# Expert weights prepared in half tiles, row factors stored as rows, and the preparation of the second layer moved, in a transform, mixture-of-experts and MLP kernel

## The chip, the cores and the metric

The kernel runs on one core of a Trainium2 chip. The metric is the device time of one execution in microseconds. Engines are named as the profile names them: PE (TensorE matmul), PEld (its weight loads), DVE (VectorE), ACT (ScalarE), POOL (GpSimd) and SP (SyncE, which here issues nearly all plain DMAs).

## What is computed

The reference takes x of 8 x 3072 x 256 and does three things in a row: a two-dimensional Fourier transform per batch of which the real part is kept, a mixture of eight experts with one expert per token, and a dense two-layer MLP.

```python
X = np.fft.fft(np.fft.fft(x, axis=1), axis=2).real          # 24576 tokens of 256
logits = x @ w_gate; expert_idx = argmax(logits)             # one expert of 8 per token
out[mask] = gate_w[mask, None] * (relu(xe @ w1[e]) @ w2[e])  # 256 -> 1024 -> 256
h = x @ w_in                                                 # 256 -> 2048
g = where(h >= 1, h, where(h <= -1, 0, (h + 1)**2 / 4))
return g @ w_out                                             # 2048 -> 256
```

## The kernel before

Matmuls of the two feed-forward parts run in fp16, each operand split into a high and a low half, so that one product is three matmuls. Everything that feeds them has first to be scaled by a power of two and split on ACT and DVE.

**Batches.** `all_batches` walks the eight batches. For each one `stage_a` (load x, fold it on DVE, transform on PE), `stage_db` for either half of the frequencies, and `route` for either half. `route` computes the gates, scales and splits the rows into `zsp` and `zsm` tiles and scatters them on POOL into the table `zd` in HBM, sorted by expert (`scatter`, line 564, 32 scatters in each batch). `table` then writes a list of tiles (`steps`): which rows of `zd`, which expert. A `yield` in these generators is one step of the main stream.

**Tiles of rows.** `Moe.run` takes the steps one by one. A tile has 128 to 512 rows. It is loaded transposed (`load_z`), goes through both expert layers in eight rounds of `l1` and `l2`, and each round yields twice, 16 yields a tile. The seven tiles of the first two batches (`PLAN[0]` four of 256 rows, `PLAN[1]` three of 512) are "raw": their expert weights are read as fp32 from the inputs and their matmuls run in fp32. All later tiles read split fp16 weights from `wd`, which `weights` writes. At the end of a tile `store` (line 811) sends the transposed result to `ytd` and the row factors `gs` (gate probability times scales, one number per row, one row per partition) to `gd`.

**Expert weights.** `weights` runs once, after the tables of batch 1 and before `stage_a` of batch 2. For each of eight experts it loads the two matrices (1 MB each) into three buffers borrowed from `xt` and `z`, takes the largest magnitude of one on DVE (line 270) and of the other by an accumulating ACT pass (line 274, its output goes to a `uv` buffer that nobody reads), makes the scales through two tiny matmuls (`all_max`), then makes four split pieces (lines 247 and 248) in the two `uv` buffers and stores each in `wd` (line 249). The load of a matrix waits until a whole earlier matrix has been split.

**MLP.** `Mlp.prep` prepares the dense layer's weights: for each of the two matrices 8 chunks (a load `mh`, then five DVE passes and three on `mlp.eng`, 5 yields), the largest magnitude, the scale, and 16 split steps: 66 yields for one matrix, 132 in all. `Mlp.run` works on blocks of 512 rows, 16 rounds of two yields, and can begin only when `prep` is over. `load` fetches a block (`ml`, `mg`), `factors` multiplies by the row factors on POOL (line 1018), `absmax` and the scales follow a block ahead.

**What sets the order.** SP's order is that of the program, the other engines' order is laid out at compile time from the same program. At the bottom (lines 1259 to 1296) the streams are interleaved by hand: until the first steps exist only the main stream and `prep` (0.3 of its steps for one main step, from the eleventh on) are drawn; then, as long as `prep` lasts, one tile yield is followed by `RAWF` main steps and `RAWP` prep steps (the first numbers until the steps of batch 1 exist, the second after that); then tile yields, MLP yields and main steps (1.25 after each of the two, 2.2 where no tile is ready). After the preparation PSUM gives the transform a single bank.

```python
                while not steps:
                    if len(fft.scattered) and mlp.eng is G:
                        mlp.eng = V
                    next(main)
                    i += 1
                    if i > PREPA:
                        ready(PREP0)
...
            while due[1]:
                i = len(steps) >= RAW
                if next(rows) == "wait":
                    forth(WAIT, 2)
                    ready(WAIT)
                else:
                    forth(RAWF[i], 2)
                    ready(RAWP[i])
```

Of the kernel before, what the change touches and what calls it, by code (L numbers as in the profile page):

```python
# [27 lines left out]
ZW = 258  # L28
# [20 lines left out]
RAWP = (0.7, 2.4)  # L49
# [109 lines left out]
def tile_kernel(ctx: ExitStack, tc: tile.TileContext, x, wg, w1, w2, win, wout,  # L159
# [56 lines left out]
    dis = [const.tile([128, 4], I32, name=f"di{i}") for i in range(NBLK)]  # L216
# [16 lines left out]
    def weights(pool, ps, later):  # L233

        def split(e, part, k, t):
            s = sct[:, e, part:part + 1]
            w = pool.tile([128, 2, 4, 128], F32, tag="uv", name="uv", bufs=2).rearrange("p a b c -> p (a b c)").bitcast(F16)
            w = w.rearrange("p (a b f) -> p a b f", a=2, b=2)
            if part == 0:

                src = t.rearrange("p (c f) -> p c f", c=2)[:, :, 512 * k:512 * k + 512]
                hi, lo = w[:, :, 0], w[:, :, 1]
            else:

                src = t.rearrange("p (j f) -> p j f", j=4)[:, 2 * k:2 * k + 2]
                hi, lo = w[:, 0], w[:, 1]
# [4 lines left out]
        ts = {}  # L251

        def load(j):
            if j >= 2 * E:
                return
            e, part = divmod(j, 2)
            t = pool.tile([128, 9 if j % 3 == 2 else 8, D], F32, tag=("xt", "xt", "z")[j % 3], name="wa", bufs=(2, 2, 1)[j % 3])
            t = ts[j] = t.rearrange("p a b -> p (a b)")[:, :2048]
            Y.dma_start(t.rearrange("p (c f) -> p c f", c=8 if part else 2), w2_view(e) if part else w1_view(e))

        load(0)
        load(1)
        store = None
        for e in range(E):
            for i in range(12 if e == 0 else 2):
                if e == 0 and i == 10:
                    load(2)
                yield
            am = pool.tile([128, 2], F32, name="wam", tag="wam", bufs=2)
            keep(V.tensor_reduce(am[:, 0:1], ts[2 * e], axis=AX.X, op=ALU.max, apply_absolute_value=True))  # L270
            yield

            ab = pool.tile([128, 2, 4, 128], F32, tag="uv", name="uv", bufs=2).rearrange("p a b c -> p (a b c)").bitcast(F16)
            keep(A.activation(ab, ts[2 * e + 1], AF.Abs, accum_out=am[:, 1:2]))
            for _ in range(4):
                yield
            pp = pool.tile([128, 2], F32, name="wpp", tag="wpp", bufs=2)
            for _ in all_max(am, 2, ps, later, pp):
                for _ in range(3):
                    yield  # L280
# [5 lines left out]
            for part in range(2):  # L286
                for k in range(2):
                    if store:
                        store()
                    store = split(e, part, k, ts[2 * e + part])  # L290
                    yield
                if part:
                    store()
                    store = None
                load(2 * e + part + 3)
# [381 lines left out]
    class Moe:  # L677
        def __init__(self, pool):
            self.pool = pool
            self.st = {}  # L680
            self.rows = self.stored = 0
            self.over = False
# [46 lines left out]
        def scale(self, n):  # L729
            st = self.st[n]  # L730
            nt, mt = st["nt"], st["mt"]
            st["gs"] = small.tile([128, 4], F32, tag="gs", name="gs", bufs=4)
            keep(V.tensor_scalar(st["gs"][:, :nt], mt[:, :, 1], st["sc"], None, op0=ALU.mult))
            if nt > 1:
                keep(V.tensor_copy(dis[st["blk"]][:, st["j"]:st["j"] + nt], mt[:, :, 0]))
# [143 lines left out]
    class Mlp:  # L879
# [117 lines left out]
        def load(self, t):  # L997
# [3 lines left out]
            if t < NBLK:  # L1001
# [4 lines left out]
                st["di"] = dis[t]  # L1006
# [160 lines left out]
    with tc.manual_schedule(engines={mybir.EngineType.SP}):  # L1167
# [37 lines left out]
        def all_batches():  # L1205
            yield from fft.stage_a(0)
            for b in range(B):
# [9 lines left out]
                if b == 1:  # L1217
                    yield from tables(b)
                    yield from weights(fpool, lambda shape: fft.ps("fb", shape), lambda fn: fft.later("w", fn))
# [27 lines left out]
        with tc.tile_pool(name="mlpp", bufs=1, side="right") as ppool:  # L1247
# [80 lines left out]
```

## Time and profile before

| | us |
|---|---|
| median of three runs | 3614.98 |
| the three runs | 3614.57, 3614.98, 3622.17 |
| the profiled execution | 3629.25 |
| its span | 3627.5 |
| PE busy in the span | 3389.2 |
| DVE, ACT, POOL busy | 2283.5, 1748.5, 1602.7 |

Busy time is the union of an engine's instructions; for PE the ends of matmuls are modelled. The profiled execution lies 14.3 us above the median of the runs. Its span is the sum of PE's busy time and PE's idle time, and the stages differ in how the two divide, so the views are read by stage. The cuts used below are moments of this execution: 47 is the first scatter of the first batch, 105 its last, 197 the last matmuls of the raw tiles of the first batch, 248 the end of the MLP's preparation, 336 the last raw matmul, 445 the last store of expert weights, 611 the first matmul of a tile with split weights.

### The profile page before, as it was taken

How to read it: one execution, taken by the hardware profiler on the slowest of the kernel's cores; microseconds unless marked ns; L12 is line 12 of the kernel's file. 1: busy time of each engine (PE TensorE's matmuls, PEld its weight loads, DVE VectorE, ACT ScalarE, POOL GpSimd, SP SyncE). 2: the span in 40 equal slices, each digit the busy share in tenths (PEclk: the TensorE clock that was granted, in tenths of full speed). 3: DMA queues.
4: the chain of work that ended last, by engine and by line, in shares of the span. 5: the costliest groups of instructions: out<-in, count | busy, mean ns of one | idle time of the engine just before them, and what ended most of it. 6: DMA issues, size and time to landing. Idle time of an engine off the chain costs nothing.

```text
span 3627.5 us, 60272 instructions
## 1 busy us (share of the span) xinstructions
PE 3389.2 (93%) x21741; PEld 2183.5 (60%) x21741; DVE 2283.5 (63%) x5137; ACT 1748.5 (48%) x3256; POOL 1602.7 (44%) x1399
## 2 busy tenths in 40 slices
PE   4778878998999999998999999999999999999999
PEld 4644545555565555555555566667777776666676
DVE  8566865676656666556544455566666666667676
ACT  3435644454444444444444444445444545555555
POOL 5442543343333433343432234344545445666555
PEclk7889988999999999999999999999999999999999
DMA  4677522544443533343444354344434441000000
GB/s 160 149 199 211 188 89 79 133 104 110 108 104 98 115 107 88 104 97 88 113 97 88 88 104 108 101 105 104 115 103 120 111 109 41 30 30 30 32 27 19
DMA packets 278608, 363.21 MB, mean 100 GB/s; under 512 B 172737, under 2 KB 193090, under 8 KB 275236
## 3 DMA queue, kind: packets, MB, share of 16 engines
q1 hardware_dynamic: 255028, 304.84, 33.2%
q0 software_dynamic: 23280, 54.52, 5.1%
q8 instruction: 171, 2.80, 0.3%
q14 instruction: 129, 1.06, 0.1%
HBM read 238.24 MB, written 95.87 MB: 92 GB/s over the span
## 4 chain that ended last, share of the span: by engine, by line
PE 70%; DVE 15%; issue 6%; DMA 3%; ACT 3%; POOL 2%; SPq 0%; another core or an unknown queue 0%; POOLq 0%; DVEq 0%; ACTq 0%
PE l L1057 21%; PE po L1086 18%; PE l L760 11%; PE py L799 9%; PE py L1086 4%; DVE r L1069 3%; DVE gf L1071 2%; ACT r L1068 1%; POOL g L1046 1%; DMA xt<-in_x 1%; PE py L780 1%; DMA wd<-uv 1%; PE f L425 1%; PE f L433 1%; DVE zam L520 1%
## 5 line engine op out<-in xcount | busy, mean ns | idle before, releaser
L1046 POOL TENSOR_TENSOR g<-gf,g 128x512 f16<-128x512 f32 (+1 forms) x784 | 925.9, 1182 | 1565.4 <-ACT g L1045 1525.8
L1057 PE MATMUL l<-yt,mw 128*128 128x512 f16 (+1 forms) x4704 | 1138.6, 377 | 23.7 <-issue 14.9
L1069 DVE SCALAR_TENSOR_TENSOR r<-r,bw 128x512 f32<-128x512 f32 (+1 forms) x784 | 657.8, 839 | 672.4 <-ACT r L1068 655.4
L1086 PEld LDWEIGHTS <-g 128*128 128x128 f16 x9216 | 898.5, 98 | 246.0 <-POOL g L1046 31.3
L1086 PE MATMUL po<-mw,g 128*128 128x256 f16 x7872 | 986.1, 274 | 26.9 <-POOL g L1046 23.0
L1068 ACT ACTIVATE r<-l,bw 128x512 f32<-128x512 f32 (+1 forms) x784 | 601.3, 767 | 549.2 <-PE l L1057 516.6
L1045 ACT CAST g<-gf 128x512 f16<-128x512 f32 (+1 forms) x784 | 474.9, 606 | 648.2 <-DVE gf L1071 620.6
L1057 PEld LDWEIGHTS <-mw 128*128 128x128 f16 x4704 | 457.4, 98 | 458.5 <-issue 46.5
L1071 DVE SCALAR_TENSOR_TENSOR gf<-l,bw,r 128x512 f32<-128x512 f32 (+1 forms) x784 | 577.4, 737 | 63.6 <-DVE r L1069 2.3
L760 PE MATMUL l<-zt,w 128*128 128x512 f16 (+2 forms) x3072 | 560.3, 318 | 27.3 <-DVE gf L1071 22.6
L799 PE MATMUL py<-h,w 128*128 128x512 f16 (+1 forms) x2064 | 472.9, 363 | 2.5 <-issue 2.5
L760 PEld LDWEIGHTS <-w 128*128 128x128 f16 x3072 | 272.2, 98 | 236.2 <-issue 43.5
L766 DVE SCALAR_TENSOR_TENSOR h<-l,h 128x512 f16<-128x512 f32 (+2 forms) x512 | 267.9, 523 | 224.0 <-ACT h L765 211.5
L765 ACT ACTIVATE h<-l 128x512 f16<-128x512 f32 (+2 forms) x512 | 238.1, 465 | 216.1 <-PE l L760 198.0
L799 PEld LDWEIGHTS <-w 128*128 128x128 f16 x2064 | 201.4, 98 | 181.7 <-issue 6.4
L1102 POOL DMA_INDIRECT out<-mo,di x178 | 189.1, 1062 | 89.4 <-ACT mo L1094 43.5
L564 POOL DMA_INDIRECT zd<-zsp,pi x136 | 147.2, 1083 | 171.5 <-ACT zsm L557 41.6
L1086 PE MATMUL py<-mw,g 128*128 128x256 f16 x1344 | 165.0, 273 | 0.0
L1018 POOL TENSOR_TENSOR ml<-ml,mg 128x512 f32<-128x512 f32 (+1 forms) x90 | 120.4, 1353 | 77.7 <-DMA mg<-gd 56.5
L564 POOL DMA_INDIRECT zd<-zsm,pi x120 | 124.3, 1036 | 53.9 <-issue 28.3
L796 PE MATMUL py<-h,w 128*128 128x256 f32 (+1 forms) x224 | 82.3, 493 | 17.0 <-ACT h L755 10.2
L754 PE MATMUL l<-zt,w 128*128 128x256 f32 (+1 forms) x224 | 84.6, 504 | 13.3 <-DVE zt L825 13.3
(256 smaller groups left out, 2491.9 us busy)
## 6 DMA issues: line engine op xcount, KB each, us to landing
w<-wd SPq DMA_DIRECT2D x256, 512.0 KB
ml<-yt SPq DMA_DIRECT2D x44, 512.0 KB
yt<-y SPq DMA_DIRECT2D x78, 256.0 KB
xt<-in_x SPq DMA_DIRECT2D x16, 1024.0 KB
wa<-in_w SPq DMA_DIRECT2D x16, 1024.0 KB
wd<-uv SPq DMA_DIRECT2D x32, 512.0 KB
w<-in_w SPq DMA_DIRECT2D x28, 512.0 KB
mg<-gd SPq DMA_DIRECT2D x44, 256.0 KB
```

The costliest lines, as they stand in the source:

```text
L564: i = G.indirect_dma_start(out=zd[:, :], out_offset=bass.IndirectOffsetOnAxis(ap=idx, axis=0), in_=rows, in_offset=None, bounds_check=ZROW ...
L760: P.matmul(ph, w[:, c, a, sl], zt[:, zz, c, :m], start=k == 0, stop=k == 5)
L765: A.activation(hi, ph, AF.Relu)
L766: V.scalar_tensor_tensor(lo, ph, 0.0, hi, op0=ALU.max, op1=ALU.subtract)
L799: P.matmul(st["py"][c], w[:, a, o + 128 * c:o + 128 * c + 128], h[:, r, :m], start=f == 0 and k == 0, stop=f == 7 and k == 2)
L1045: A.copy(hi, gf)
L1046: G.tensor_tensor(lo, gf, hi, op=ALU.subtract)
L1057: P.matmul(ph, w[:, a, sl], yt[:, b, c, :m], start=k == 0, stop=k == 5)
L1068: A.activation(r, ph, AF.Relu, bias=st["b1"], scale=st["c1"])
L1069: V.scalar_tensor_tensor(r, r, st["mc"], r, op0=ALU.min, op1=ALU.mult)
L1071: V.scalar_tensor_tensor(gf, ph, st["c2"], r, op0=ALU.mult, op1=ALU.max)
L1086: P.matmul(po, g[:, a, js], w[:, b, sl], start=f == 0 and k == 0 and j % 2 == 0, stop=f == 15 and k == 2, skip_group_check=True)
```

## The change

- **Row factors.** `gs` becomes one of four lasting 128 x 32 tiles that are cleared once. After the factors are computed in its first columns, DVE transposes it in blocks of 32 into `gt`, so that factors of 32 partitions lie in one row; `store` then writes them with four DMAs of rows of 32 numbers in place of one DMA of single numbers. The row indices `dis` become one tile in place of one per block.
- **Expert weights.** The three buffers become eight slots of half a matrix (six in `xt` and `z`, two in the transform's `au`). The load, the magnitude and the split go by halves. The magnitudes of an expert alternate with the splits of the expert before it; a half is loaded two experts ahead as soon as its slot has been split. The unread output of the magnitude pass goes to a `zsp` buffer instead of `uv`. Counted in the code, the generator has 122 yields in place of 154.
- **Preparation.** None between the first scatter of the first batch and its table. After that 1.0 and 3.0 prep steps for a tile yield in place of 0.7 and 2.4; the three passes of `mlp.eng` run on DVE until the steps of batch 1 exist and on POOL after that (before: DVE during the first batch's scatters, POOL otherwise).

```diff
-RAWP = (0.7, 2.4)
+RAWP = (1.0, 3.0)
...
+        slots = []
+        for tag, n, w in (("xt", 2, 8), ("xt", 2, 8), ("z", 1, 9)):
+            v = f1(pool.tile([128, w, D], F32, tag=tag, name="wa", bufs=n), 2)
+            slots += [v[:, 0], v[:, 1]]
+        slots += [a.rearrange("d g s c -> d (g s c)")[:, :1024] for a in fft.au]
...
+            if e < E:
+                k, part = divmod(i, 2)
+                t = slots[(4 * e + i) % 8]
+                if part == 0:
+                    Y.dma_start(t.rearrange("p (c f) -> p c f", c=2), w1_view(e)[:, :, 512 * k:512 * k + 512])
+                else:
+                    Y.dma_start(t.rearrange("p (c d) -> p c d", c=4), w2_view(e)[:, 4 * k:4 * k + 4])
...
+        for i in range(4):
+            load(0, i)
+        yield
+        for i in range(4):
+            load(1, i)
+            yield
...
+        for e in range(E + 1):
+            am = pool.tile([128, 2, 2], F32, name="wam", tag="wam", bufs=2)
+            for i in range(4):
+                if e < E:
+                    src = slots[(4 * e + i) % 8]
+                    if i % 2 == 0:
+                        keep(V.tensor_reduce(am[:, i // 2, 0:1], src, axis=AX.X, op=ALU.max, apply_absolute_value=True))
+                    else:
+                        keep(A.activation(ab, src, AF.Abs, accum_out=am[:, i // 2, 1:2]))
                 yield
+                if store:
+                    store()
+                    store = None
+                if e > 0:
+                    store = split(e - 1, i)
+                    yield
+                    load(e + 1, i)
...
-            st["gs"] = small.tile([128, 4], F32, tag="gs", name="gs", bufs=4)
+            st["gs"] = self.gs[n % len(self.gs)]
...
+                st["gt"] = small.tile([128, 32], F32, tag="gt", name="gt", bufs=2)
+                keep(V.transpose(st["gt"], st["gs"]))
...
-            Y.dma_start(gd[blk][0, o:o + m].rearrange("(j p) -> p j", p=128), st["gs"][:, :nt])
+            for b in range(4):
+                Y.dma_start(gd[blk][0, o:o + m].rearrange("(j b q) -> b j q", b=4, q=32)[b], st["gt"][32 * b:32 * b + nt])
...
-                    if len(fft.scattered) and mlp.eng is G:
-                        mlp.eng = V
                     next(main)
                     i += 1
-                    if i > PREPA:
+                    if i > PREPA and not fft.scattered:
                         ready(PREP0)
...
-            mlp.eng = G
             while due[1]:
                 i = len(steps) >= RAW
+
+                mlp.eng = G if i else V
```

## Rows read from the trace of the kernel before

**Rows 1.** The page, PE's busy share in 40 slices of the span (tenths):

```profile
PE   4778878998999999998999999999999999999999
```

**Rows 2.** Busy time by stage: stretch, its length, each engine, granted clock, DMA:

```profile
47.00:105.00 58.00, 26.11 (x117) 22.38 (x116) 52.17 (x182) 23.54 (x65) 48.37 (x32) 0.56 0.35 109
105.00:197.00 92.00, 71.70 (x348) 61.09 (x349) 56.74 (x236) 42.10 (x126) 39.24 (x35) 0.89 0.71 165
197.00:248.00 51.00, 33.97 (x83) 16.75 (x82) 30.54 (x45) 12.27 (x22) 30.02 (x22) 0.80 0.86 221
248.00:336.00 88.00, 79.60 (x258) 36.37 (x257) 54.25 (x107) 44.91 (x61) 15.92 (x12) 0.96 0.69 207
336.00:445.00 109.00, 89.81 (x545) 54.85 (x544) 91.07 (x132) 68.78 (x94) 50.10 (x36) 0.96 0.56 177
445.00:611.00 166.00, 126.29 (x791) 86.20 (x790) 106.50 (x306) 77.39 (x169) 84.90 (x75) 0.88 0.26 84
611.00:911.00 300.00, 277.59 (x1556) 159.79 (x1556) 187.80 (x484) 138.16 (x284) 108.60 (x101) 0.96 0.50 119
911.00:3627.00 2716.00, 2659.15 (x17896) 1722.71 (x17893) 1671.65 (x3553) 1325.62 (x2395) 1216.17 (x1075) 1.00 0.34 86
```

**Rows 3.** POOL in order of time, 45 to 110, start, length, and idle before:

```profile
47.18 1.78 POOL L564 DMA_INDIRECT zd<-zsm,pi  x1 [10.55 <-ACT pd L428]
...
84.90 4.97 POOL L564 DMA_INDIRECT zd<-zsm,pi  x1 [0.30 <-issue]
...
104.28 0.92 POOL L564 DMA_INDIRECT zd<-zsm,pi  x1 [0.30 <-issue]
```

**Rows 4.** Groups of DVE instructions by line, 45 to 108 (the preparation's):

```profile
L922 DVE TENSOR_REDUCE mam<-mr 128x1 f32<-128x1024 f32 x4 | 4.8, 1207 | 0.0
...
L918 DVE TENSOR_TENSOR mr<-mr,mm 128x512 f32<-128x512 f32 x6 | 4.1, 682 | 0.0
...
L911 DVE TENSOR_SCALAR mp<-mu 128x512 uint32<-128x512 uint32 x5 | 2.1, 414 | 0.0
```

**Rows 5.** Groups of POOL instructions by line, 130 to 206 (the second batch's scatters):

```profile
L564 POOL DMA_INDIRECT zd<-zsp,pi x17 | 18.8, 1106 | 48.2 <-ACT zsp L545 38.3 <-DVE zsp L540 5.8 <-issue 3.7
L564 POOL DMA_INDIRECT zd<-zsm,pi x15 | 14.3, 953 | 4.4 <-issue 3.8 <-ACT zsp L545 0.3 <-ACT zsm L557 0.3
...
L917 POOL TENSOR_TENSOR mr<-mr,mu 128x512 f32<-128x512 f32 x3 | 3.8, 1278 | 0.5 <-DVE mr L915 0.5
```

**Rows 6.** Who waited for whom, 105 to 255: total, times, longest:

```profile
DVE mu L908 <- DMA mh<-in_wout: 16.9, 2, 16.2
...
PE l L754 <- DVE zt L825: 13.3, 1, 13.3
```

**Rows 7.** The chain that ended last, 105 to 245: start, us, what:

```profile
160.80 5.11 DMA mh<-in_wout
197.99 14.57 DMA mh<-in_wout
```

**Rows 8.** The chain that ended last, 240 to 460: the stores of expert weights on it:

```profile
260.60 8.19 DMA wd<-uv
291.94 9.70 DMA wd<-uv
...
335.99 10.44 DMA wd<-uv
```

**Rows 9.** What SP's queue waited for, 230 to 620:

```profile
SPq L249 <- DVE uv L248: 126.1, 21, 12.1
SPq L1004 <- DVE yt L1037: 53.1, 1, 53.1
```

**Rows 10.** Instructions on the row factors `gs`: duration ns min/median/max, first and last start:

```profile
L733 DVE TENSOR_SCALAR gs<-mt,stb x64: 192/217/1756, 615.4 to 2998.8; 128x4 f32<-128x4 f32 x36, 128x1 f32<-128x1 f32 x21, 128x2 f32<-128x2 f32 x7
L816 SPq DMA_DIRECT2D gd<-gs x50: 346/454/936, 137.1 to 2988.0; - x50
```

**Rows 11.** What SP's queue waited for in the whole span, the longest total:

```profile
SPq L723 <- PE py L799: 718.2, 74, 23.8
```

More of the change, by code (lines that the diff above doesn't have):

```diff
@@ L215, in tile_kernel @@
     onesf = const.tile([128, 128], F32, name="onesf")
-    dis = [const.tile([128, 4], I32, name=f"di{i}") for i in range(NBLK)]
+    dis = const.tile([128, NBLK, 4], I32, name="dis")
     V.memset(onesf, 1.0)
@@ L231, in w2_view, with weights, load, split @@
         return w2[e].rearrange("(c p) d -> p c d", p=128)
-    def weights(pool, ps, later):
-        def split(e, part, k, t):
+    def weights(fft, ps, later):
+        pool = fft.pool
+        f1 = lambda t, n: t.rearrange("p a b -> p (a b)")[:, :1024 * n].rearrange("p (n f) -> p n f", n=n)
+        slots = []
[3 more added lines that the diff above has]
+        slots += [a.rearrange("d g s c -> d (g s c)")[:, :1024] for a in fft.au]
+        def load(e, i):
+            if e < E:
[5 more added lines that the diff above has]
+                    Y.dma_start(t.rearrange("p (c d) -> p c d", c=4), w2_view(e)[:, 4 * k:4 * k + 4])
+        def split(e, i):
+            k, part = divmod(i, 2)
             s = sct[:, e, part:part + 1]
+            src = slots[(4 * e + i) % 8].rearrange("p (a f) -> p a f", a=2)
             w = pool.tile([128, 2, 4, 128], F32, tag="uv", name="uv", bufs=2).rearrange("p a b c -> p (a b c)").bitcast(F16)
             w = w.rearrange("p (a b f) -> p a b f", a=2, b=2)
[L239 to L246, printed above, removed]
+            hi, lo = (w[:, :, 0], w[:, :, 1]) if part == 0 else (w[:, 0], w[:, 1])
             A.activation(hi, src, AF.Copy, scale=s)
@@ L249, in split @@
             return lambda: Y.dma_start(wd[e, part, k], w.rearrange("p a b f -> p (a b f)"))
[L251 to L259, printed above, removed]
@@ L261, in weights @@
-        load(0)
-        load(1)
-        store = None
[L264 to L267, printed above, removed]
-                yield
-            am = pool.tile([128, 2], F32, name="wam", tag="wam", bufs=2)
-            keep(V.tensor_reduce(am[:, 0:1], ts[2 * e], axis=AX.X, op=ALU.max, apply_absolute_value=True))
+        for i in range(4):
[4 more added lines that the diff above has]
+            yield
@@ new lines, in weights @@
+        ab = pool.tile([128, 3, ZW], F32, tag="zsp", name="zsp", bufs=3).rearrange("p a b -> p (a b)")[:, :512].bitcast(F16)
+        store = None
+        for e in range(E + 1):
[7 more added lines that the diff above has]
+                        keep(A.activation(ab, src, AF.Abs, accum_out=am[:, i // 2, 1:2]))
+                yield
+                if store:
[5 more added lines that the diff above has]
+                    load(e + 1, i)
+            if e == E:
+                break
+            a2 = pool.tile([128, 2], F32, name="wa2", tag="wa2", bufs=2)
+            V.tensor_tensor(a2, am[:, 0], am[:, 1], op=ALU.max)
@@ L271, in weights @@
             yield
-            ab = pool.tile([128, 2, 4, 128], F32, tag="uv", name="uv", bufs=2).rearrange("p a b c -> p (a b c)").bitcast(F16)
-            keep(A.activation(ab, ts[2 * e + 1], AF.Abs, accum_out=am[:, 1:2]))
-            for _ in range(4):
+            pp = pool.tile([128, 2], F32, name="wpp", tag="wpp", bufs=2)
+            for _ in all_max(a2, 2, ps, later, pp):
                 yield
[L277 to L280, printed above, removed]
+                yield
@@ L285, in weights @@
             yield
[L286 to L295, printed above, removed]
+        store()
+        yield
     class Fft:
@@ L681, in __init__ @@
             self.rows = self.stored = 0
+            self.gs = [const.tile([128, 32], F32, name=f"gs{i}") for i in range(4)]
+            for t in self.gs:
+                V.memset(t, 0.0)
             self.over = False
@@ L731, in scale @@
             nt, mt = st["nt"], st["mt"]
-            st["gs"] = small.tile([128, 4], F32, tag="gs", name="gs", bufs=4)
+            st["gs"] = self.gs[n % len(self.gs)]
             keep(V.tensor_scalar(st["gs"][:, :nt], mt[:, :, 1], st["sc"], None, op0=ALU.mult))
             if nt > 1:
-                keep(V.tensor_copy(dis[st["blk"]][:, st["j"]:st["j"] + nt], mt[:, :, 0]))
+                keep(V.tensor_copy(dis[:, st["blk"], st["j"]:st["j"] + nt], mt[:, :, 0]))
+                st["gt"] = small.tile([128, 32], F32, tag="gt", name="gt", bufs=2)
+                keep(V.transpose(st["gt"], st["gs"]))
             else:
@@ L1005, in load @@
                 Y.dma_start(st["gr"][:, :m], gd[t][:, :m].to_broadcast([128, m]))
-                st["di"] = dis[t]
+                st["di"] = dis[:, t]
             else:
@@ L1218, in all_batches @@
                     yield from tables(b)
-                    yield from weights(fpool, lambda shape: fft.ps("fb", shape), lambda fn: fft.later("w", fn))
+                    yield from weights(fft, lambda shape: fft.ps("fb", shape), lambda fn: fft.later("w", fn))
                     fft.load_x(b + 1, 0)
```

## Prediction

> **What bounds the kernel now.** I read the 40 slices first, then busy time by stage, and after that only the stages with a gap. PE is at nine tenths or more from the eleventh slice on [rows 1]; from 911 to the end it works 2659.2 of 2716 us at full clock [rows 2]. Since the span is PE's busy time and PE's idle time, 3389.2 + 238.3, and the change takes no matmul of weight away, the sum below goes by PE's idle time alone. By stage it is: up to 47, 22 (47 less the 25.0 that the other stages leave of 3389.2); 47 to 105, 31.9; 105 to 197, 20.3; 197 to 248, 17.0; 248 to 336, 8.4; 336 to 445, 19.2; 445 to 611, 39.7; 611 to 911, 22.4; after that 56.9 [rows 2]. The reader is to see there that all three edits with any weight touch the first 445 us, and that each stage waits for something else.
>
> From 47 to 105 PE has little to do; the first batch's 32 scatters run on POOL almost without a break, 0.30 us apart, from 47.2 to 105.2, but they last 0.92 us at best and up to 4.97 us [rows 3]. DVE is busy 52.2 of the 58 us [rows 2], over half of it with the MLP's preparation: nine groups from 4.8 to 2.1 us, in sum 28.9 us [rows 4]. From 105 to 248 the raw tiles, the second batch and the rest of the preparation share DVE, and DMA is busy 0.71 to 0.86 of the time [rows 2]; DVE stood 16.9 us for two loads of the preparation, PE 13.3 us for the sum of a raw tile's halves on DVE [rows 6], and those two loads, 5.1 and 14.6 us, lie on the chain [rows 7]. From 248 to 445 the expert weights are made; four stores of pieces, from 8.2 to 10.4 us and one of 3.0, in sum 31.4 us, lie on the chain [rows 8], because the next user of a `uv` buffer waits until its store has landed.
>
> **The change part by part.**
>
> *A. No preparation between the first batch's scatters.* Main steps counted in the code: 171 until the first table, 55 until the first scatter. At 0.3 from the eleventh on, 48 prep steps lie there now and 13 will; 35 move behind. Without DVE's 28.9 us, 23.3 us of DVE are left in the stretch [rows 2, 4], ACT has 23.5 and PE 26.1 [rows 2]; so POOL's scatters at their best pace, 32 x (0.92 + 0.30) = 39.0 us, are what is late next. That is 19.0 us under the 58.0 measured. The second batch's scatters, with less DVE work beside them, lasted (18.8 + 14.3) / 32 = 1.03 us [rows 5], which gives 32 x 1.33 = 42.6 us and a gain of 15.4. Bounds: 8 (half, if the 13 steps that stay drag into the scatters) to 19. I take 16: the row of the second batch is the nearest.
>
> *B. The moved steps.* 35 prep steps are 7 chunks' worth of work, of which the absolute maxima are a part; chunk loads behind 105 go from 8 to about 13. The second rate is 3.0, so prep ends after about 73 tile yields (50 x 1.0 + 23 x 3.0 on top of 13) where it now ends after 71 (50 x 0.7 + 20.4 x 2.4 on top of 48). Mlp's first block therefore starts at the same place in the program. DVE gets 28.9 us more between 105 and 248, where it has 35.3 + 20.5 = 55.8 us free [rows 2]; that is the cover. If it were gone the cost would be all 28.9. POOL is relieved of prep passes between the second batch's scatters (three passes of 1.3 us [rows 5] between the last of them), so the low bound is -4. Between them I go by the row on what the preparation costs there today: 16.9 us of DVE waiting for 8 chunks [rows 6], 2.1 each, and 5 more chunks: +10.
>
> *C. Expert weights.* Five uses of the two `uv` buffers for an expert become four, and between two splits there is now a magnitude pass of the next expert, so a store has one pass more in which to land. Loads come by halves, two experts ahead. The generator takes 122 main steps in place of 154; the MLP rounds that no longer fit beside it are done later and are PE work either way. So the gain is PE's idle time from 248 to 445, 8.4 + 19.2 = 27.6 us, and at most the clock's loss on top, 0.04 x 169.4 = 6.8 us [rows 2]. The chain's 31.4 us of stores says the same size [rows 8]. Bounds 8 (one of the four stores gone) to 35; I take 24, most of the idle time, as a chain of splits remains. The change adds a wait: SP stands at each load until its slot has been split, with the tiles' weights, the MLP's block loads and the stores queued behind it. It already stands 126.1 us in 21 waits at the stores for the same DVE pass [rows 9], so the new wait takes the place of the old one: 0, bounds 0 to +10.
>
> *D. What follows.* The second transform (445 to 611) has one PSUM bank and is paced by its own latencies. Its 39.7 us of PE idle, and the 53.1 us that SP stood at one block load until DVE had freed the block [rows 9], are not touched: 0, bounds -12 to +12 as the loads fall otherwise.
>
> *E. Row factors.* 50 transposes: a DVE pass over four columns takes 0.217 us [rows 10], one over 512 columns 0.68 us [rows 4], so 11 to 34 us of DVE in all, of which nearly everything lies behind 611, where DVE is idle 1156 us [rows 2]. 50 stores of 0.454 us become 200: 68 us more on SP [rows 10], which stands 718.2 us for one kind of wait alone [rows 11]. Nothing of either is on the path: 0, bounds -5 (blocks get their factors sooner) to +5. The single index tile, the clears and the `zsp` buffer are counted at nothing: one write a tile, as before.
>
> On E the Trainium skill speaks against the change: "DMA: Bandwidth & Descriptors", section "Rules for kernel authors", says that a DMA whose outermost dimension is below 16 is confined to at most that many DMA engines, and these have four rows or two. Its section "Specifications" puts about 0.6 us of latency ahead of the first byte of a DMA from SP; by that 150 more DMAs, one behind the other on the path, would be 90 us and the time 3675. No row here shows SP or PE waiting for a store of factors.
>
> **Sum.** -16 + 10 - 24 + 0 + 0 = -30 us. The profiled span of 3627.5 becomes 3597.5. The profiled execution is 14.3 us above the median of the runs, so the median of 3615 becomes 3585.
>
> **The rivals.**
>
> *Slower: the preparation outruns its loads.* In the second half of the raw tiles 8 chunks are asked for in 13 tile yields, two buffers deep, behind raw weights and 4 MB of expert weights that are now asked for at once, where DMA is already 0.86 busy [rows 2]. If DVE stood for each of the eight at the mean of the two rows, (5.1 + 14.6) / 2 = 9.9 us [rows 7], that is 79 us in place of 16.9, and as DVE runs in order the sums of raw tiles and the second batch stand behind it. Then B is +62 in place of +10: -16 + 62 - 24 = +22, 3637. It decides from 57 us of DVE waiting for `mh` on (16.9 and the 40 that A and C bring). For it: PE's 13.3 us wait. Against: six of the eight chunks today cost nothing visible.
>
> *The stretch moves to the second batch.* DVE's passes lengthen POOL's scatters; in the first raw tiles 50 prep steps, now with all passes on DVE, run beside the second batch's 32 scatters. If these went from 1.03 us to the first batch's 48.6 / 32 = 1.52 us (POOL's 48.4 us busy [rows 2] and a remainder at the edge), 32 x 0.49 = 16 us come back, since PE's wait of 13.3 us is for the first tile of that batch [rows 6]: -14, 3601. The Trainium skill, "SBUF — State Buffer", section "SBUF: two separate sides", says why it could be so: while DVE holds the port pair that it shares with GpSimd, the latter cannot write descriptors. The long scatter between 84.9 and 89.9 [rows 3] agrees.
>
> *Given back.* The second transform keeps its distance to a block load that comes late, as the one of 53.1 us did [rows 9]; the 30 us turn into idle time between 445 and 611: 3615.
>
> *More.* The weights' stage ends early enough that the second transform meets fuller MLP work, and a third of the 39.7 + 22.4 us idle from 445 to 911 goes too [rows 2]: -30 - 21 - 9 (B at +1) = -60, 3555.
>
> *It doesn't do what it says:* the compiler's order might put preparation between the scatters all the same. That is A at 0 with B at 0, -24: 3591, inside the forecast's own range.
>
> **How the numbers follow.** Forecast, 3565 to 3600: 0.42. More: 0.13. The stretch moves: 0.15. Given back: 0.12. Slower: 0.18. 0.2% is about 7 us, what a measurement of this kernel can tell from no change. Faster is 0.42 + 0.13 + 0.15 = 0.70, same 0.12, slower 0.18. The range goes from 3545, past the center of "more", to 3633, just short of the center of the slower case; about 0.05 is left out below and 0.10 above. The forecast's own range with its bounds (A 8 to 19, C 8 to 35) is 3560 to 3608.
>
> **What would show it.** A: the last of the first 32 scatters ends near 90 (right: 86 to 92), each near 1 us. B: DVE's wait for `mh` under 30 us, and the MLP's first round no more than 10 us later than before. C: `wd` stores under 15 us on the chain, and the last store of weights 30 to 55 us before 445. D: from the last store to the first split-weight matmul 166 us as before. E: no wait that names `gd`, `gt` or `gs` beyond a few us. I would be wrong if DVE stood over 57 us for `mh`, if the second batch's scatters averaged 1.5 us, or if the distance from the last weight store to the first split-weight tile grew by 20 us or more.

## The result and the profile after

| | before | after |
|---|---|---|
| median of the runs, us | 3614.78 | 3566.96 |
| lowest to highest | 3613.76 to 3622.17 | 3565.16 to 3568.72 |
| ratio, 95% interval | | 0.9863 [0.9846, 0.988] |
| span of the profiled execution | 3627.5 | 3562.8 |
| PE busy, PE idle in it | 3389.2, 238.3 | 3377.1, 185.7 |

The kernel became 48 us faster by the medians, 1.37% by the ratio. The forecast was 3585, with a range from 3545 to 3633. The number held; most of its reasons did not, as the experiments show. The two profiled executions lie 65 us apart, more than the medians, because that of before was itself 14 us above its median.

The page of after: span, busy time of PE, PE's slices (they answer [rows 1]), packets, and the queue of SP's DMAs.

```profile
span 3562.8 us, 60571 instructions
...
PE 3377.1 (95%) x21741; PEld 2183.5 (61%) x21741; DVE 2303.6 (65%) x5207; ACT 1752.5 (49%) x3272; POOL 1592.2 (45%) x1399
...
PE   5778788999999999999999999999999999999999
...
DMA packets 259777, 363.21 MB, mean 102 GB/s; under 512 B 150833, under 2 KB 171186, under 8 KB 257428
...
q1 hardware_dynamic: 236196, 304.84, 29.8%
```

The bytes are what they were, 363.21 MB, but there are 18,831 packets fewer (278,608 before), and the time that SP's packets took fell from 33.2% of the engines' span to 29.8%.

Busy time of after by stage, cut at the moments that answer those of [rows 2]: the columns are length, then PE, PE's weight loads, DVE, ACT, POOL, granted clock, DMA share and GB/s.

```profile
47.00:91.00 44.00, 27.53 (x153) 24.14 (x152) 32.60 (x147) 25.15 (x75) 33.78 (x32) 0.75 0.33 97
91.00:187.00 96.00, 73.00 (x331) 61.60 (x332) 64.68 (x252) 41.59 (x120) 35.08 (x32) 0.88 0.68 198
187.00:248.00 61.00, 44.40 (x102) 19.68 (x100) 50.50 (x80) 16.61 (x28) 37.64 (x26) 0.83 0.60 184
248.00:312.00 64.00, 59.36 (x203) 27.93 (x204) 43.09 (x85) 38.56 (x59) 11.87 (x9) 1.00 0.80 255
312.00:407.00 95.00, 74.71 (x450) 45.51 (x449) 81.00 (x125) 59.89 (x85) 37.69 (x29) 0.96 0.62 208
407.00:588.00 181.00, 146.47 (x884) 99.52 (x882) 126.19 (x335) 88.71 (x184) 93.27 (x80) 0.88 0.24 76
588.00:888.00 300.00, 288.15 (x1669) 168.21 (x1670) 194.96 (x507) 147.85 (x298) 120.35 (x108) 1.00 0.44 125
888.00:3562.00 2674.00, 2638.68 (x17803) 1713.82 (x17800) 1678.36 (x3577) 1318.89 (x2384) 1213.19 (x1071) 1.00 0.31 87
```

PE's idle time by stage is 16.5, 23.0, 16.6, 4.6, 20.3, 34.5, 11.9 and 35.3 us, where before had 31.9, 20.3, 17.0, 8.4, 19.2, 39.7, 22.4 and 56.9. The forecast looked for its 30 us ahead of 445. There the scatters' stretch gives 15.4, and the four stages behind it 0.4 together. The transform gives 5.2, the 300 us after it 10.5, and the long rest 21.6, where neither the preparation nor the expert weights are at work any more. The only edit that still acts there is the one of the row factors, counted at nothing. PE's busy time fell by 12.1 us with the same 21741 matmuls; in the 300 us after the transform the granted clock is 1.00 where it was 0.96. Counted by PE's matmuls, after leads before by 12 us at the 800th (286 us into before), 16 at the 1400th (425), 22 at the 2400th (635), 39 at the 4000th (937), 61 at the 9000th (1833) and 65 at the end.

The row factors of after: the four stores a tile (SP) and the transposes (DVE); count, then shortest, median and longest in ns, and first and last start. They answer [rows 10].

```profile
L835 SPq DMA_DIRECT2D gd<-gt x200: 228/320/1157, 131.9 to 2924.3; - x100
L753 DVE STREAM_TRANSPOSE gt<-gs x50: 189/211/214, 99.7 to 2889.1; 128x32 f32<-128x32 f32 x50
```

SP's part is 200 x 0.32 = 64 us in place of 50 x 0.454 = 23, and the transposes are 10.6 us of DVE. So the edit adds work on both engines, and yet the stretch in which it acts became shorter.

### The profile page after: what moved, and what is told of

The parts are those of the page before. It is cut to its first block, busy times and chain, and to the rows that moved or that the text cites. A ratio compares the mean times of both kernels' runs of the same rounds, so it can differ in the third digit from the quotient of the medians.

```text
span 3562.8 us, 60571 instructions
## 1 busy us (share of the span) xinstructions
PE 3377.1 (95%) x21741; PEld 2183.5 (61%) x21741; DVE 2303.6 (65%) x5207; ACT 1752.5 (49%) x3272; POOL 1592.2 (45%) x1399
## 2 busy tenths in 40 slices
DMA packets 259777, 363.21 MB, mean 102 GB/s; under 512 B 150833, under 2 KB 171186, under 8 KB 257428
## 3 DMA queue, kind: packets, MB, share of 16 engines
q1 hardware_dynamic: 236196, 304.84, 29.8%
q14 instruction: 131, 1.07, 0.1%
## 4 chain that ended last, share of the span: by engine, by line
PE 72%; DVE 13%; issue 5%; DMA 4%; ACT 3%; POOL 3%; SPq 0%; POOLq 0%; DVEq 0%; ACTq 0%
PE l L1076 22%; PE po L1105 18%; PE l L778 11%; PE py L817 10%; PE py L1105 4%; DVE r L1088 3%; DVE gf L1090 2%; POOL g L1065 1%; DMA wd<-uv 1%; ACT r L1087 1%; PE f L421 1%; PE py L798 1%; DMA zd<-zsm,pi 1%; POOL zd L576 1%; DVE zam L532 1%
## 5 line engine op out<-in xcount | busy, mean ns | idle before, releaser
L1088 DVE SCALAR_TENSOR_TENSOR r<-r,bw 128x512 f32<-128x512 f32 (+1 forms) x784 | 667.0, 851 | 657.4 <-ACT r L1087 655.8
L778 PE MATMUL l<-zt,w 128*128 128x512 f16 (+2 forms) x3072 | 556.7, 316 | 14.2 <-DVE gf L1090 11.9
L1121 POOL DMA_INDIRECT out<-mo,dis x178 | 187.8, 1055 | 93.5 <-ACT mo L1113 47.7
L1056 DVE SCALAR_TENSOR_TENSOR yt<-ml,bw,yt 128x512 f16<-128x512 f32 (+1 forms) x90 | 74.4, 845 | 28.5 <-ACT yt L1055 28.3
```

The costliest lines, as they stand in the source:

```text
L778: P.matmul(ph, w[:, c, a, sl], zt[:, zz, c, :m], start=k == 0, stop=k == 5)
L1088: V.scalar_tensor_tensor(r, r, st["mc"], r, op0=ALU.min, op1=ALU.mult)
```

## The experiments

They ran in three sets on three chips, each beside the kernel before on the same chip (medians 3624.01, 3632.79 and 3614.18). Ratios are to those; times of different sets are only compared through them. Even so a comparison across sets can be off by more than its interval: the kernel before differs by 19 us from chip to chip, while the kernels with the rows lie close together on two of them (3566 for the rows alone on one, 3563 and 3567 with more reads and with spread numbers on the other).

**Which part carries the gain.** Four kernels: the preparation's new order alone (A and B of the prediction), the expert weights alone (C), the rows alone (E), and everything but the rows.

*The rows alone:* the index tile, the lasting `gs`, the transpose and this store.

```diff
-            Y.dma_start(gd[blk][0, o:o + m].rearrange("(j p) -> p j", p=128), st["gs"][:, :nt])
+            for b in range(4):
+                Y.dma_start(gd[blk][0, o:o + m].rearrange("(j b q) -> b j q", b=4, q=32)[b], st["gt"][32 * b:32 * b + nt])
```

> The kernel before with the row factors' part alone: lasting gs tiles, DVE transposes, four row DMAs a tile, one index tile. Theory (the parts add up, and the row factors are worth nothing): 3610 to 3620 us, within 0.2% of the kernel before. Rival (the PE idle time that went after the first split-weight tile, 32 us between the two profiles, is the row factors'): 3575 to 3600 us, with POOL waiting less for mg and PE's idle time after 611 down from 79 to about 50 us.

Measured: 3565.74 us (3561.32 to 3567.82), ratio 0.9838 [0.9822, 0.9854], below even the rival's range. The whole gain is here. PE's idle time is 189.8 us in place of 238.3. At PE's matmuls its lead over before is 27 us at the 1400th (425 us into before), 30 at the 2400th, 41 at the 4000th, 61 at the 9000th and 64 at the end, so that less than half of it comes ahead of the 445 us in which the forecast looked.

*The preparation's order alone:*

```diff
-RAWP = (0.7, 2.4)
+RAWP = (1.0, 3.0)
...
-                    if len(fft.scattered) and mlp.eng is G:
-                        mlp.eng = V
...
-                    if i > PREPA:
+                    if i > PREPA and not fft.scattered:
...
+                mlp.eng = G if i else V
```

> The kernel before with the preparation's part alone: none between the first batch's scatters, 1.0 and 3.0 steps after that, its three passes on DVE until the second batch's steps exist. Theory: the last of the first 32 scatters ends near 91 instead of 105 us, and about 10 us of the 14 are lost again while the raw tiles share DVE and DMA with the moved steps: 3605 to 3612 us. Rival 1 (the whole 14 us arrive at the end): 3600 us. Rival 2 (all given back in the raw tiles): 3615 us or more, with the MLP's first round no earlier than 278 us.

Measured: 3641.12 us, ratio 1.0047 [1.0031, 1.0063]. As the second rival had it, 3615 or more; that rival does not say why the kernel is 17 us slower than before and not level with it.

*The expert weights alone* (with one line more, `fft.flush("w")`, that issues the stage's pending work ahead of the scales; the change has no such line):

```diff
-    def weights(pool, ps, later):
+    def weights(fft, ps, later):
...
+        slots += [a.rearrange("d g s c -> d (g s c)")[:, :1024] for a in fft.au]
...
+            fft.flush("w")
             sc = sct[:, e]
```

> The kernel before with the expert weights' part alone: halves through eight slots, 122 main steps in place of 154 (and one flush of pending evacuations ahead of the scales). Theory: this is the largest part, 3580 to 3595 us, the last weight store 25 to 40 us earlier than 445. Rival (the stage ends earlier but the time is lost between the last store and the first split-weight tile): last store as early, that distance longer than 162 us by 20 or more, time 3605 or more.

Measured: 3636.78 us, ratio 1.0036 [1.0022, 1.0051]: slower too, as the rival had it, though with smaller distances than it named. The line `fft.flush("w")` was not run by itself, so its price is not known.

*Both without the rows:* the diff of the change without the five places that name `gs`, `gt` and `dis`.

> The changed kernel with the row factors as before (single numbers in one DMA, no transpose): preparation and weights parts together. Theory: 3562 to 3572 us, the changed kernel's time, as the row factors are worth nothing. Rival (the row factors matter in the steady stretch): 3580 to 3600 us.

Measured: 3628.54 us, ratio 1.001 [1.0, 1.0019]. Neither theory nor rival: the two edits on which the forecast stood make no difference of use.

**What in the rows.** A look back at the chain of before gave the theory. Three DMAs on it last 13 us and more, and each is under way behind a store of factors: those stores start at 137.1 (0.1 us after the first of the three), 190.6 and 838.4. First the chain of before at two places (the third of them, a load of 14.57 us at 197.99, is in [rows 7]), then SP's queue at the later one:

```profile
137.03 13.12 DMA zd<-zsp,pi
...
838.89 13.97 DMA xt<-in_x
```

```profile
838.39 0.44 SPq L816 DMA_DIRECT2D gd<-gs  x1
838.89 1.37 SPq L380 DMA_DIRECT2D xt<-in_x  x2
```

In the kernel with the rows alone the load of `xt` on the chain between 760 and 860 takes 6.74 us. The old store writes 512 numbers of 4 bytes for a large tile, 22,872 more 4-byte packets in the whole trace than with rows (44,229 to 21,357), and the new one pieces of 128 bytes. The two kernels side by side, 2 us each, from 2 us behind the third store on: GB/s is the last column, the busy share of the DMA engines the one ahead of it. A packet's whole time is booked in the slice in which it starts, so that a share can pass 1.

Before, store at 190.6:

```profile
192.60:194.60 2.00, 2.00 (x8) 1.61 (x7) 2.00 (x8) 0.82 (x4) 1.52 (x3) 0.69 1.25 66
194.60:196.60 2.00, 2.00 (x11) 1.77 (x10) 1.80 (x16) 0.38 (x1) 1.70 (x2) 1.00 1.04 41
196.60:198.60 2.00, 2.00 (x11) 1.77 (x10) 0.00 (x0) 0.38 (x1) 1.68 (x3) 1.00 1.18 41
198.60:200.60 2.00, 2.00 (x11) 1.77 (x10) 0.00 (x0) 0.51 (x2) 1.83 (x2) 1.00 0.62 33
```

The rows alone, store at 178.8:

```profile
180.80:182.80 2.00, 2.00 (x11) 1.77 (x10) 2.00 (x11) 0.61 (x2) 1.97 (x2) 1.00 0.69 142
182.80:184.80 2.00, 2.00 (x11) 1.75 (x10) 1.16 (x11) 0.38 (x1) 1.63 (x2) 1.00 0.95 385
184.80:186.80 2.00, 2.00 (x11) 1.76 (x10) 0.00 (x0) 0.38 (x1) 1.59 (x2) 1.00 1.03 368
186.80:188.80 2.00, 2.00 (x11) 1.77 (x10) 0.00 (x0) 0.38 (x1) 1.67 (x3) 1.00 1.06 381
```

The reader is to see that the DMA engines count as busy in both (1.18 and 1.03), while 41 GB/s go through in the one and 368 in the other. A busy share says only that packets are under way. From this came the theory that the large packets behind the store are held up.

*The old store beside the new one,* into a tensor that nothing reads:

```diff
+            Y.dma_start(gx[blk][0, o:o + m].rearrange("(j p) -> p j", p=128), st["gs"][:, :nt])
```

> The kernel with the rows alone (3566 us), and the old store number by number kept beside the new one, into a tensor that nothing reads. Theory (the 4-byte writes of a factor store hold up what is queued behind them on the DMA engines): the gain goes again, 3608 to 3632 us, and large packets behind these stores are as slow as in the kernel before. Rival (the gain comes from the lasting factor tiles, the single index tile, or from factors that land sooner): still 3560 to 3574.

Measured: 3641.11 us, ratio 1.0029 [1.0009, 1.005], against the 0.9838 of the rows alone. The store by single numbers takes the whole gain back by itself; nothing that the new layout brings makes up for it.

*The rest of the edit without its store:* lasting `gs` and one index tile, but the old store.

> The lasting factor tiles and the single index tile alone, without the transpose, and with the old store number by number. Theory: nothing of the gain is here, 3608 to 3632 us. Rival (they carry the gain, since a small tile's turn no longer waits for an old store): 3560 to 3580.

Measured: 3629.06 us, ratio 0.9999 [0.9986, 1.0013]. The tiles are worth nothing; the rival falls.

*The same bytes in fewer pieces:*

```diff
-            Y.dma_start(gd[blk][0, o:o + m].rearrange("(j p) -> p j", p=128), st["gs"][:, :nt])
+            Y.dma_start(gd[blk][0, o:o + m].rearrange("(p j) -> p j", p=128), st["gs"][:, :nt])
```

> The kernel before with one store of factors a tile as before and the same bytes, but partition by partition: 128 writes of 16 bytes in place of 512 of 4. The factors so land in another order, and the sum at the end weighs rows with each other's factors; the work is otherwise the same. Theory, if the price goes by the number of writes: a quarter of the 58 us is left, 3570 to 3592 us. Rival, if it goes by the store as such or by its bytes: 3610 to 3632, as before.

Measured: 3584.42 us, ratio 0.9875 [0.9844, 0.9906]. As expected: one DMA a tile as before, 2 KB as before, 128 writes in place of 512, and about three quarters of the gain is there (by the intervals, from a half to nearly all). The price is that of small writes, not of the store.

*A second dose:* the kernel before, with the line that `rows_plus_numbers` adds (a store of single numbers into `gx`) behind its own store.

> The kernel before with the store of the factors number by number made twice, the second into a tensor that nothing reads. Theory: a second dose of the same hold-up, 30 to 65 us on top of the kernel before, 3645 to 3690 us. Rival (the store itself costs nothing): within 8 us of the kernel before.

Measured: 3638.96 us, ratio 1.0029 [1.0013, 1.0046], some 10 us on top (5 to 17 by the interval) where 30 to 65 were expected. The theory in this form fell: twice the writes don't hold up twice as long. The window behind one store shows it. In before, 6 us behind the store at 1038.7:

```profile
1044.70:1046.70 2.00, 2.00 (x11) 0.94 (x10) 0.03 (x1) 1.05 (x2) 1.16 (x1) 1.00 0.00 0
1046.70:1048.70 2.00, 2.00 (x13) 1.02 (x12) 1.27 (x2) 0.78 (x1) 0.00 (x0) 1.00 1.76 33
1048.70:1050.70 2.00, 2.00 (x17) 1.49 (x15) 1.18 (x3) 0.62 (x1) 0.28 (x1) 1.00 0.39 33
1050.70:1052.70 2.00, 2.00 (x12) 1.08 (x10) 0.61 (x1) 0.60 (x2) 0.87 (x1) 1.00 0.56 197
```

With both stores, the same tile, store at 1042.5:

```profile
1048.50:1050.50 2.00, 2.00 (x11) 0.94 (x10) 0.51 (x1) 0.60 (x1) 1.16 (x1) 1.00 0.70 25
1050.50:1052.50 2.00, 2.00 (x15) 1.21 (x13) 1.17 (x3) 0.78 (x1) 0.00 (x0) 1.00 1.03 16
1052.50:1054.50 2.00, 2.00 (x15) 1.25 (x13) 0.81 (x2) 0.62 (x1) 0.75 (x1) 1.00 0.51 57
1054.50:1056.50 2.00, 2.00 (x12) 1.11 (x11) 0.69 (x1) 1.08 (x2) 0.41 (x1) 1.00 0.47 172
```

The slow stretch is three slices in place of two, not four. PE is busy in all of them, so nothing is lost on PE in these 8 us; where the price of the stores falls is read off PE's lead with the rows alone, above. The mean over all 50 stores, worked out from the packets of 1 KB and more in each trace (GB/s, by us behind the store):

| us behind the store (rows alone: behind the first of its four DMAs) | 4 to 6 | 6 to 8 | 8 to 10 | 10 to 12 | 12 to 14 |
|---|---|---|---|---|---|
| before | 50 | 29 | 45 | 97 | 193 |
| numbers twice | 44 | 25 | 32 | 73 | 184 |
| 16 bytes each | 68 | 124 | 147 | 99 | 111 |
| rows alone | 109 | 117 | 130 | 95 | 115 |
| rows, and numbers 512 bytes apart | 134 | 145 | 95 | 100 | 109 |

So the writes of two stores into two tensors seem to go side by side, and those of one store to wait for each other. What the 512 of one store share is a stretch of 2 KB. The last row of the table is the experiment on that.

*The same numbers, spread out:* as many 4-byte writes as in the first of these kernels.

```diff
+    gx = [dram.tile([512, 128], F32, name=f"gx{i}") for i in range(NBLK)]
...
+            Y.dma_start(gx[blk][o:o + m, 0].rearrange("(j p) -> p j", p=128), st["gs"][:, :nt])
```

> The rows alone, and beside the new store the old one number by number into a tensor that nothing reads, but with 512 bytes between one number and the next. As many writes of 4 bytes as in rows_plus_numbers (3641 us); only their neighbourhood is gone. Theory 1 (any 4-byte write costs): 3615 to 3645 us. Theory 2 (writes next to each other wait for one another at the memory, which is also why a second store into another tensor added only 6 to 10 us): 3562 to 3585 us, and 4 to 11 us after such a store the DMA engines move over 90 GB/s in place of 30 to 50.

Measured: 3566.57 us, ratio 0.9871 [0.9856, 0.9886]. Theory 2: the writes are nearly free where they are 512 bytes apart. By the medians the kernel is within 1 us of the rows alone, by the ratios 0.33% above it, on another chip; a rest of up to some 0.5%, against 1.91% with the numbers side by side, is not excluded. Those packets of 1 KB and more that take over three times the median of their size within 14 us of a store of single numbers add up to 32 us of the 16 engines' time, and to 199 us with the numbers side by side. It is neighbouring 4-byte writes that hold up the queues. The Trainium skill, "DMA: Bandwidth & Descriptors", section "Specifications", says that a transfer under 512 bytes is done as a read, a change and a write. Two such writes that meet in one place would have to take turns; the result agrees with that, but no run shows the turns themselves. By the size alone the spread writes and the 128-byte pieces would be as dear, and 0.9871 and 0.9838 say that they are not.

*Reads of that size:* the rows alone with each tile's pairs of numbers, 512 reads of 8 bytes, loaded twice.

```diff
+            mx = small.tile([128, 4, 2], F32, tag="mx", name="mx", bufs=4)[:, :nt]
...
+                       Y.dma_start(mx, rows[:, 256:258].rearrange("(j p) d -> p j d", p=128))):
```

> The rows alone, with every tile's two numbers a row (512 reads of 8 bytes each for a large tile) loaded a second time into a tile that nothing uses. Theory (writes alone hold up): 3562 to 3575 us. Rival (any small piece does): 3590 to 3625 us.

Measured: 3562.8 us, ratio 0.986 [0.9845, 0.9875]. These reads cost nothing that can be seen. They lie a row of `zd` apart, 258 numbers or 1032 bytes, so reads side by side remain untried.

**Do the other two edits pay once the stores are gone?** The rows with the preparation's order, and the rows with the expert weights:

> The rows and the preparation's new order, without the new expert weights. Theory (the order costs as much as it did alone, 12 to 22 us): 3574 to 3590 us, ratio 0.987 to 0.990. Rival (it cost only because the stores held up the loads behind it, and now gives what was forecast for it): 3552 to 3564, ratio 0.981 to 0.983.

Measured: 3574.59 us (3572.52 to 3579.26), ratio 0.9895 [0.988, 0.991]. The theory: it costs as much as alone.

> The rows and the new expert weights, with the preparation as before. Theory (they cost as much as they did alone, 8 to 18 us): 3572 to 3588 us, ratio 0.986 to 0.990. Rival (they give the 24 us of the forecast once the stores are gone): 3538 to 3555, ratio 0.977 to 0.981.

Measured: 3556.61 us (3549.26 to 3557.51), ratio 0.9837 [0.9823, 0.985]. Neither: by the ratios nothing is lost or won over the 0.9838 of the rows alone, by the medians 9 us are won, on another chip. This kernel has the line `fft.flush("w")` too.

So the effect of each edit, alone and beside the others, in per cent of the kernel before (differences of the ratios; the two columns with the rows go across sets and carry both intervals, some 0.2 each way, and the difference of the chips). A star marks an entry in which the line `fft.flush("w")` comes or goes as well:

| | alone | with the one other | with the rows | with the rows and the other |
|---|---|---|---|---|
| preparation (A, B) | +0.47 | -0.26* | +0.57 | +0.26* |
| expert weights (C) | +0.36* | -0.37 | -0.01* | -0.32 |

The entries without a star agree with each other: the preparation's order costs about 0.5%, and the expert weights give about 0.35% beside it. The starred ones differ from them by 0.7% without the rows and 0.3% with them. Either the two edits get in each other's way or the added line has that price; no run tells these apart. The stage of the expert weights lasts 177.5 us with the line and 175.7 without it (`weights_only`, `no_rows`), so a price would have to fall behind it.

The rows: -1.62 alone, -1.52 beside A, -1.99 beside C, -1.47 beside both. The rows with the expert weights, and the rows alone, both read 0.25% below the change as made; the intervals touch, so that this is likely and not settled. On one chip the kernel without the moved preparation stood 18 us below the one without the expert weights.

## Why the prediction was right, and where its steps were wrong

**The number.** The sum said -30, and the ratio gives -50 on 3615: the forecast of 3585 was 18 us off, inside the range. That it came so near was luck: it came about by two errors. The terms that were to bring the gain, -16 + 10 - 24, measured +0.1% together without the rows. The term put at 0 measured -53 to -72 us (1.47 to 1.99% of 3615). The sum also went by PE's idle time alone, and 12.1 of the 65 us between the profiles are busy time. Two smaller slips stand in it: the nineteenth slice of [rows 1] is at 8, not 9, so that idle time was to be seen behind the first 445 us too; and with B at +10 the bounds of A and C give 3571 to 3609, not 3560 to 3608.

**E, the step that failed.** "Nothing of either is on the path: 0, bounds -5 (...) to +5." The prediction costed what the edit adds, on DVE and SP, and was right there: 10.6 us of transposes against "11 to 34", 41 us more on SP against 68, all hidden. It did not cost what the edit takes away. Of the old store it took the 0.454 us on SP for its price, but that is the issue; the price was on the DMA engines, in the packets behind. The rows were in hand: a load of the preparation of 14.57 us [rows 7], 7 us behind a store of factors, was read as DMA being full, and made the price of the *slower* rival. The view for it is the window behind a store with share and GB/s side by side. The test named for E, a wait that names `gd` or `gs`, could not show it either: who waits then waits for `xt`, `mh`, `wd` or the scatters. Nor did the 90 us come, the time of 3675, that were worked out from the first-byte latency in the Trainium skill, "DMA: Bandwidth & Descriptors", section "Specifications": the kernel with 200 stores of four rows or two ran in 3566. The rule on the outermost dimension in the Trainium skill, "DMA: Bandwidth & Descriptors", section "Rules for kernel authors", shows no price in that time either.

**A: the scatters moved as forecast, and the lead was all but gone when the MLP began.** After's last scatter of the first 32, POOL in order of time, answers [rows 3]:

```profile
89.34 0.92 POOL L576 DMA_INDIRECT zd<-zsm,pi  x1 [0.30 <-issue]
90.57 0.92 POOL L576 DMA_INDIRECT zd<-zsm,pi  x1 [0.30 <-issue]
```

It ends at 91.5, inside "86 to 92", and the scatters' mean fell from 1.52 to 1.07 us; that DVE's work beside them made them long is borne out, by which means is not shown. PE was 16 us ahead at its 200th matmul with A alone. But the first matmul of the MLP starts at 276.9 us in before and at 277.4 with A alone, at 261.6 with the rows alone and at 262.9 with the rows and A. Counted by matmuls, 2 us of the lead are left at the 800th and 6 at the 1000th, 344 us into before (with the rows 2 and 3). The preparation that the MLP waits for ended later; the lines show the splits of MLP weights on DVE, the last figure of the times the start of the last one, first before, then the rows alone, A alone, and after:

```profile
L936 DVE SCALAR_TENSOR_TENSOR mw<-mr,msc,mw x16: 736/742/751, 107.5 to 246.6; 128x512 f16<-128x512 f32 x16
```

```profile
L943 DVE SCALAR_TENSOR_TENSOR mw<-mr,msc,mw x16: 706/744/754, 102.4 to 232.1; 128x512 f16<-128x512 f32 x16
```

```profile
L936 DVE SCALAR_TENSOR_TENSOR mw<-mr,msc,mw x16: 735/742/751, 163.1 to 257.1; 128x512 f16<-128x512 f32 x16
```

```profile
L955 DVE SCALAR_TENSOR_TENSOR mw<-mr,msc,mw x16: 739/744/747, 157.5 to 247.0; 128x512 f16<-128x512 f32 x16
```

**B: +10 was right for the preparation, and the sum with A was near up to the MLP.** A alone puts the last split from 246.6 to 257.1, +10.5, as forecast; with the rows it goes from 232.1 to 242.9, +10.8. Up to the 1000th matmul the two terms made between 0 and -6, where the sum had -6. What failed of it lies behind that place, where the sum had nothing (below). The rows bring 14.5 us at this point by themselves, with three factor stores (137.1 to 190.6) among its loads. The *slower* rival asked for 57 us of waiting for `mh`; DVE waited 9.9 in after [rows 6]:

```profile
DVE mu L927 <- DMA mh<-in_wout: 9.9, 4, 4.4
```

The second batch's scatters, the other rival, averaged (21.3 + 14.7) / 32 = 1.13 us in after against 1.03 [rows 5]: 3 us, not 16.

**C: PE's idle time did not go, work was put off.** The stage ends sooner, but the stores did not leave the chain. After, the chain from 225 to 430, the stores of expert weights, against [rows 8]:

```profile
249.54 6.62 DMA wd<-uv
...
293.75 7.47 DMA wd<-uv
...
304.40 4.27 DMA wd<-uv
...
310.43 7.84 DMA wd<-uv
```

There are eight of them there, 45.6 us in sum, where under 15 were promised (before had 31.4 in four). The last store of expert weights starts at 444.7 in before, at 427.9 with C alone, at 413.0 with the rows alone and at 391.5 with both; first and last start, the rows alone and then both:

```profile
L249 SPq DMA_DIRECT2D wd<-uv x32: 327/337/1382, 242.6 to 413.0; - x32
```

```profile
L264 SPq DMA_DIRECT2D wd<-uv x32: 332/504/1429, 236.7 to 391.5; - x32
```

So the stage ends 17 and 21.5 us sooner, near the 24 of the forecast. In after the last store is at 407.3, 38 ahead of before's and inside the "30 to 55". But "the gain is PE's idle time from 248 to 445" is the step of C that failed. With C alone the MLP's matmuls give way in the stage and come back behind it. The lines hold PE's instructions on `mw` alone, from 248 to the last store of weights and from there to the first matmul of a tile with split weights; the figure behind the length is the time of its matmuls. First before, then C alone:

```profile
248.00:445.00 197.00, 103.21 (x627) 21.97 (x222) 0.00 (x0) 0.00 (x0) 0.96 0.62 190
445.00:611.00 166.00, 90.60 (x527) 16.83 (x162) 0.00 (x0) 0.00 (x0) 0.88 0.26 84
```

```profile
248.00:427.90 179.90, 84.11 (x484) 17.66 (x174) 0.00 (x0) 0.00 (x0) 0.91 0.75 200
427.90:606.80 178.90, 111.46 (x643) 21.24 (x210) 0.00 (x0) 0.00 (x0) 0.91 0.24 77
```

19 us of MLP work leave the first stretch and 21 come into the second. PE's idle time from the first to the last of these stores is 27.6 us in before and 32.1 with C alone, 31.5 with A and 37.0 with A and C, 17.6 with the rows, 15.6 with the rows and C, 21.5 with the rows and A and 23.4 in after: C lowers it in one pair of four, by 2 us. So **D**, "166 us as before", fails: the second stretch is 179 us with C alone, 176 with the rows and C against 170 without C, and 181 in after. Its idle time of 39.7 us was not touched, as forecast: it is 35 to 43 in all of them. Of the 17 us 5 were left at the first split-weight matmul, and none at the end, as the rival *given back* had it for all three edits. The prediction had counted the deferred rounds as "PE work either way", and still took the stage's length for gain. Why the kernels with A or C alone lose more behind that place is open (PE's lag is 3 us at the 2000th matmul and 13 at the 9000th with A, 2 at the 2400th and 6 at the end with C).

## What to carry to other kernels

Cost what an edit takes away on the DMA engines as carefully as what it adds to the instruction queues: the price of these small writes was seen in the GB/s of the microseconds behind them, not in their own rows. Numbers that lie one to a partition are better turned on chip and stored as rows; where that can't be, places far apart did nearly as well here, and fewer and longer pieces most of it. An early lead is not yet a gain: look for it again at the next point that waits for something else, as the 16 us of A that were all but gone when the MLP began. And where PE bounds the kernel, a stage that ends sooner has won only as much as PE's idle time in it fell.

## What was not expected of the hardware

512 writes of 4 bytes into one stretch of 2 KB held the DMA engines at 29 to 50 GB/s from 4 to 10 us behind the store, at a busy share of up to 1.76, where 109 to 130 GB/s went through without them; fifty such stores made 58 us of 3624 (the kernel before and the rows alone, on one chip). The packets of 4 bytes show a median of 9 ns themselves in every one of these kernels; the time is recorded on the large packets behind them, 2028 of which (1 KB and more) took over three times the median of their size within 14 us of a store, against 897 with the rows. Two such stores into two tensors overlapped (10 us for the second). 16-byte pieces left about a quarter of the price; 4-byte writes 512 bytes apart left little or none (0.9871 to 0.9838 across chips), and 8-byte reads 1032 bytes apart none that shows. From what distance on it is free, and whether neighbouring small reads cost the same, was not tried.
